# One written table orders all work of an attention and maxout-MoE kernel

## The chip, the cores and the metric

The kernel runs on one core of a Trainium2 chip. The core has five engines that run side by side, each with its own queue in program order: PE (TensorE, matmuls into PSUM), VectorE (DVE in the profile), ACT (ScalarE), POOL (GpSimd) and SP (SyncE, which here only issues DMAs). POOL can issue DMAs too, and those may change the type on the way. An instruction waits for semaphores of the others; whatever stands behind it on its engine waits with it. The metric is the device time of one execution in microseconds.

## The reference

```python
def _attn_ref(q, k, v):                 # (8 batches, 8 heads, 576 rows, 64)
    scores = (1 / np.sqrt(64)) * np.matmul(q, k.transpose(0, 1, 3, 2))
    mask = (pos[:, None] // 64) >= (pos[None, :] // 64)      # causal by blocks of 64
    attn = softmax(np.where(mask, scores, -1e9))
    return np.matmul(attn, v)

x = attn_out.transpose(0, 2, 1, 3).reshape(4608, 512)
h1, h2 = x @ w1, x @ w2                  # 512 -> 1024
out = np.maximum(h1, h2) @ w_out         # 1024 -> 512, float32
```

The kernel uses max(h1, h2) = relu(x (w1 - w2)) + x w2. So out = g w_out + x M with g = relu(x d), d = w1 - w2 and M = w2 w_out. M costs a small matmul of weights once; after that a row needs x d and one product of [x g] (1536 long) with [M; w_out].

## The kernel before, in words

**Attention** goes by pairs of heads, 32 pairs, two to a group. A group's q and k are loaded as fp32 (`load_qk`), cast to bf16 (`cast`), transposed on PE (`transposes`, 18 small ones) and copied out of PSUM to `qT` and `kT`. From group 6 on k comes by casting DMAs of POOL (`load_blocks`) and DMA transposes of SP (`transpose_blocks`). A pair's scores fill tiles of 2 x 512 columns in `ps_s` (two buffers of PSUM); ACT takes the exponential of each into `aT` (L568; L624 for a corner), POOL or VectorE sets masked corners to zero (`mask`, L573), and PE multiplies `aT` by `vv`, which holds v and a column of ones (`av`, L652). VectorE divides by the sum (L658, L659). The four pairs of the first batch are cut differently, in four pieces (`burst_p`, `burst_q1`, `burst_q2`, `burst_q3`), so that the first 256 rows are done early. The result is transposed into `xT` by PE (`x_out`) or, from group 4 to 14, by a DMA (`x_dma`).

**MoE** goes by spans of rows: 256, 320, seven of 512, and 448 (`spans`). For each span `h_unit` makes one of eight slices of x d, four matmuls into `ps_h`, drained through relu into `g` by VectorE or ACT. As spans do not end on 128 rows, `g` carries 64 columns over to the next span with a POOL copy (L236). The last step is a 2 x 2 block product of [x g] and [M; w_out], done with seven smaller `product`s of twelve matmuls each in place of eight. These need sums and differences of weights (`weight_sums`, L358) and of rows (`row_sums`, L364), kept in four `slot`s and in `bT_sb`; odd spans have a part of the row sums in a tile `xsum` of their own. VectorE makes all of them. `after` adds the results out of PSUM into `y` and stores them from SP.

**Weights.** `load_w` loads `moe_w1` (fp32) and `moe_w2` (to bf16) from POOL's queue, `diff_w` makes d on VectorE, `bT_unit` transposes `moe_w2` on PE, `m_unit` makes M.

**What sets the order.** Attention is written out by hand, in calls. MoE work stands in a list `units`; `fill(n)` runs the next steps of it whose rows are done, about n matmuls, at the places where the hand-written part calls it. Fixed rules place the drains: a unit's sums stand right behind it (`M_SUMS`, `G_SUMS`, `X_SUMS`). Every engine executes in the order in which the calls are made.

All tiles of MoE and of transposes share four PSUM buffers (`ps_m`).

Of the kernel before, what the change touches and what calls it, by code (L numbers as in the profile page):

```python
# [14 lines left out]
def kernel(  # L15
# [10 lines left out]
    nc = tc.nc  # L26
# [31 lines left out]
    QCUT = 256  # L58

    def a_col(p, c, t):  # L60
        if p >= HP:
            return CB[c] + t * P
        late = t * P >= QCUT
        return t * P + {
            0: 384 - QCUT if late else 0, 1: 704 - QCUT if late else 256 - P,
            2: 1024 - QCUT, 3: 1408 - 3 * P, 4: 1344 - 4 * P,
        }[c]


    SPAN = 512  # L70
    spans = [(0, QCUT), (QCUT, S - QCUT)]
    spans += [(t0, min(SPAN, NTOK - t0)) for t0 in range(S, NTOK, SPAN)]
    NSPAN = len(spans)


    FAST = 2
    carry = [t0 % P for t0, _ in spans]
    tiles = [(carry[i] + w) // P for i, (_, w) in enumerate(spans)]
# [34 lines left out]
    def load_qk(g, queues, gated=False):  # L113
        b, u = divmod(g, GPB)
        for nm, src, queue in (("q", q, queues[0]), ("k", k, queues[1])):
            if queue is None or by_dma(nm, g):
                continue
            raws[nm, g] = t = raw.tile([P, 2, RPP * D], FP32, name=f"{nm}raw")
            if gated:
                nc.gpsimd.memset(t[:, 0, :1], 0.0)  # L120
            queue.dma_start(
                out=t[:],
                in_=src[b, 4 * u:4 * u + 4].rearrange(
                    "(s h) (p t) d -> (h p) s (t d)", h=2, t=RPP),
            )

    T_DMA = {nm: 6 for nm in "k"}
    blk_n = {}

    def by_dma(nm, g):  # L130
        return g >= T_DMA.get(nm, NG)

    def load_blocks(nm, g):
        b, u = divmod(g, GPB)
        blk_n[nm, g] = n = raw.tile([P, S // BLK, 2, D], BF16, name=f"{nm}b", tag=f"{nm}raw")
        for h in range(2):
            for s in range(2):
                nc.gpsimd.dma_start(  # L138
                    out=n[h * BLK:(h + 1) * BLK, :, s],
                    in_=(q if nm == "q" else k)[b, 4 * u + 2 * s + h].rearrange(  # L140
                        "(j p) d -> p j d", p=BLK),
                )

    def transpose_blocks(nm, g):
        n = blk_n.pop((nm, g))
        for h in range(2):
            nc.sync.dma_start_transpose(
                out=(qT_r if nm == "q" else kT_r)[(2 * g + h) % NT].rearrange(
                    "q (j p) -> q j p", p=BLK),
                in_=n[h * BLK:(h + 1) * BLK].rearrange("p j s d -> p (j s d)"),  # L150
            )

    def cast(nm, g, parts):
        if by_dma(nm, g):
            return
        t = raws[nm, g].rearrange("p s (t d) -> p t s d", d=D)
        if (nm, g) not in qk_n:
            qk_n[nm, g] = qkn.tile([P, RPP, 2, D], BF16, name=f"{nm}n")
        n = qk_n[nm, g]
        for copy, j0, j1 in parts:  # L160
            copy(out=n[:, j0:j1], in_=t[:, j0:j1])  # L161
# [19 lines left out]
    def load_w(j, which=(0, 1)):  # L181
        fs = slice(j * WB, (j + 1) * WB)
        if 0 in which:
            w1_raw[j] = wraw.tile([P, NDM, WB], FP32, name="w1raw")
            nc.gpsimd.dma_start(out=w1_raw[j][:], in_=w1r[:, :, fs])
        if 1 in which:
            nc.gpsimd.dma_start(out=w2_sb[j], in_=w2r[:, :, fs])

    def diff_w(j):
        fs = slice(j * WB, (j + 1) * WB)  # L190
        nc.vector.tensor_sub(d_sb[:, :, fs], w1_raw[j][:], w2_sb[j])  # L191
# [8 lines left out]
    dve, pool, act = nc.vector.tensor_copy, nc.gpsimd.tensor_copy, nc.scalar.copy  # L200
    SP, ACT = nc.sync, nc.scalar
    warm = small.tile([P, 1], FP32, name="warm")
    load_qk(0, (SP, ACT))
    nc.vector.memset(warm[:], 0.0)
    zeros = wpool.tile([P, SPAN], BF16, name="zeros")
    nc.vector.memset(zeros[:], 0.0)
    nc.scalar.activation(out=warm[:], in_=warm[:], func=AF.Exp)
    load_qk(1, (SP, SP))
    load_qk(2, (SP, None))
    make_identity(nc, ident)  # L210
    for r in range(NV):
        nc.vector.memset(vv_r[r][:, :, :, D:D + 1], 1.0)
        nc.vector.memset(vv_r[r][:BLK, NCH - 1, :, :], 0.0)
    for r in range(NA):
        nc.vector.memset(aT_r[r][:, :, AW:], 0.0)
    for r in range(NT):
        nc.vector.memset(kz_r[r][:, BLK:2 * BLK], 0.0)
    cast("q", 0, ((dve, 0, 7), (pool, 7, RPP)))
    cast("k", 0, ((act, 0, 5), (dve, 5, RPP)))
    for c in range(2):  # L220
        load_v(0, c)
    load_w(0, (0,))
    cast("q", 1, ((pool, 7, RPP),))
    cast("k", 1, ((pool, 0, 7),))
    load_w(0, (1,))


    done_tokens = [0]
    g_tiles = {}

    def h_unit(i, f):
        if f == 0:
            g_tiles[i] = g_pool.tile([P, NFF, SPAN + BLK], BF16, name="g")
            if carry[i]:
                end = carry[i - 1] + spans[i - 1][1]
                nc.gpsimd.tensor_copy(  # L236
                    out=g_tiles[i][:, :, :carry[i]],
                    in_=g_tiles[i - 1][:, :, end - carry[i]:end])
        g = g_tiles[i]
        t0, w = spans[i]  # L240
        m = carry[i]
        pt = ps_m.tile([P, SPAN], FP32, name="ps_h", tag="m")
        for c in range(NDM):
            nc.tensor.matmul(  # L244
                pt[:, :w], d_sb[:, c, f * P:(f + 1) * P], xT[:, c, t0:t0 + w],
                start=(c == 0), stop=(c == NDM - 1),
            )
            if c == NDM - 1:
                if i >= FAST and on_act(i, f):
                    nc.scalar.activation(out=g[:, f, m:m + w], in_=pt[:, :w], func=AF.Relu)  # L250
                else:
                    nc.vector.tensor_scalar_max(g[:, f, m:m + w], pt[:, :w], 0.0)  # L252
                if i in (1, *range(FAST, NSPAN)) and f in X_SUMS:
                    row_sums(i, X_SUMS[f], 0)
            yield

    def bT_unit(j):
        pt = ps_m.tile([P, 2, NDM, P], BF16, name="ps_bT", tag="m")
        for i in range(2):
            for c in range(NDM):  # L260
                nc.tensor.transpose(pt[:, i, c, :], w2_sb[j][:, c, i * P:(i + 1) * P], ident[:])  # L261
                if i == 1 and c == NDM - 1:
                    (act if j % 2 else dve)(
                        out=bT_sb[:, 2 * j:2 * j + 2, :],
                        in_=pt.rearrange("p i c d -> p i (c d)"))
                yield

    def m_unit(i, c):
        ds = slice(i * WH, (i + 1) * WH)
        pt = ps_m.tile([P, WH], FP32, name="ps_M", tag="m")  # L270
        for f in range(NFF):
# [4 lines left out]
            if f == NFF - 1:  # L276
                nc.vector.tensor_copy(out=m_sb[:, c, ds], in_=pt[:])  # L277
                for k in M_SUMS[NDM * (1 - i) + c]:
                    weight_sums(k)
            yield  # L280

    def y_terms(i, s):
        g = g_tiles[i]
        t0 = spans[i][0] - carry[i] + s * P
        return [(xT[:, c, t0:t0 + P], m_sb[:, c]) for c in range(NDM)] + [
            (g[:, f, s * P:(s + 1) * P], wo_sb[:, f]) for f in range(NFF)]

    def y_unit(i, s):
        t0 = spans[i][0] - carry[i] + s * P
        py = ps_m.tile([P, d_model], FP32, name="ps_y", tag="m")  # L290
        terms = y_terms(i, s)
        for n, (lhs, rhs) in enumerate(terms):
            nc.tensor.matmul(
                py[:], lhs, rhs, start=(n == 0), stop=(n == len(terms) - 1),
            )
            if n == len(terms) - 1:
                y = y_pool.tile([P, d_model], FP32, name="y")
                nc.vector.tensor_copy(out=y[:], in_=py[:])
                nc.sync.dma_start(out=out[t0:t0 + P, :], in_=y[:])
            yield  # L300

    def y_last(i, s):
        t0 = spans[i][0] - carry[i] + s * P
        for m, w, copy, queue in ((0, 256, act, SP), (256, P, dve, SP), (384, P, act, ACT)):
            py = ps_m.tile([P, w], FP32, name="ps_y", tag="m")
            terms = y_terms(i, s)
            for n, (lhs, rhs) in enumerate(terms):
                nc.tensor.matmul(
                    py[:], lhs, rhs[:, m:m + w], start=(n == 0), stop=(n == len(terms) - 1),
                )  # L310
                if n == len(terms) - 1:
                    y = y_pool.tile([P, d_model], FP32, name="y")
                    copy(out=y[:, :w], in_=py[:])
                    queue.dma_start(out=out[t0:t0 + P, m:m + w], in_=y[:, :w])
                yield

# [12 lines left out]
    def a_parts(i, row, half):  # L329
        j, r = (row, 0) if i == 1 else (i, row)  # L330
        g, t0 = g_tiles[j], spans[j][0] - carry[j] + 2 * r * P
# [605 lines left out]
```

## Time and profile before

| what | value |
|---|---|
| median of 3 runs | 248.3 us (247.65 to 248.72) |
| the profiled execution | 247.61 us, its span 245.8 us |
| busy: PE, VectorE, ACT, POOL | 234.4, 185.4, 143.8, 129.6 us |
| granted TensorE clock | 0.997 |
| instructions in the trace | 7595 |

The span runs from the first to the last instruction of the program. Busy time is a union: matmuls are pipelined, so one that takes 273 ns may start 109 ns after the one ahead. Idle time in the groups has the releaser beside it, the instruction that ended the wait. PEld is the weight load ahead of a matmul. The chain that ended last goes back from the last instruction, at each step to what released it.

### The profile page before, as it was taken

What the parts mean: (1) busy time and instruction counts of PE and PEld (TensorE: products, weight loads), DVE (VectorE), ACT (ScalarE), POOL (GpSimd) and SP (SyncE); (2) the same over time, 40 slices, a digit from 0 to 9 for tenths busy, and PEclk for the clock granted to TensorE, in tenths of its full rate; (3) what the DMA queues carried; (4) which work ended last, traced back from release to release, by engine and by line L of the source; (5) the groups of instructions that cost most, each with busy time, mean ns of one, the idle gap of its engine ahead of it and who ended that gap; (6) DMA issues with size and microseconds to landing.
All of it is one profiled execution on the core that took longest, in us unless ns stands there. A gap on an engine that the chain in (4) does not pass through costs nothing.

```text
span 245.8 us, 7595 instructions
## 1 busy us (share of the span) xinstructions
PE 234.4 (95%) x3093; PEld 167.3 (68%) x3109; DVE 185.4 (75%) x395; ACT 143.8 (58%) x200; POOL 129.6 (53%) x294
## 2 busy tenths in 40 slices
PE   7689899999999999999999999999999999999993
PEld 2347666688865886588558755875587578567782
DVE  4976989999677958795879587957785788526573
ACT  2888871677677748673867386748673730462200
POOL 1996952669959584948593859485621210010000
PEclk9999999999999999999999999999999999999998
DMA  6999999579999999999999999999994321301125
GB/s 233 318 206 306 231 278 195 172 137 188 153 196 180 168 163 222 184 201 183 244 227 130 208 164 272 122 223 193 134 138 97 100 39 45 131 0 43 47 86 172
DMA packets 108867, 41.33 MB, mean 168 GB/s; under 512 B 89248, under 2 KB 102688, under 8 KB 108832
## 3 DMA queue, kind: packets, MB, share of 16 engines
q0 software_dynamic: 65952, 11.87, 69.4%
q1 hardware_dynamic: 42464, 28.32, 51.7%
q10 hardware_dynamic: 416, 0.66, 0.8%
q8 instruction: 24, 0.39, 0.7%
q14 instruction: 11, 0.09, 0.1%
HBM read 34.60 MB, written 9.44 MB: 179 GB/s over the span
## 4 chain that ended last, share of the span: by engine, by line
PE 87%; DVE 7%; ACT 4%; issue 1%; ACTq 0%
PE ps_p L390 35%; PE ps_h L244 24%; PE ps_o L652 11%; PE ps_s L544 9%; PE ps_w L514 3%; ACT aT L568 3%; PE ps_qT L525 2%; DVE sums L358 2%; DVE sums L364 1%; DVE g L252 1%; DVE m_sb L277 1%; PE ps_s L562 1%; PE ps_xe L690 1%; PE ps_bT L261 1%; DVE qT L533 1%
## 5 line engine op out<-in xcount | busy, mean ns | idle before, releaser
L568 ACT ACTIVATE aT<-ps_s 128x1024 bf16<-128x1024 f32 (+2 forms) x100 | 95.7, 994 | 32.1 <-PE ps_s L544 24.0
L244 PE MATMUL ps_h<-xT,d_sb 128*128 128x512 bf16 (+3 forms) x307 | 68.0, 357 | 1.0 <-DVE d_sb L191 0.3
L573 POOL MEMSET aT<- 64x128 bf16 x124 | 21.8, 200 | 52.8 <-ACT aT L568 51.9
L244 PEld LDWEIGHTS <-d_sb 128*128 128x128 bf16 x320 | 29.7, 98 | 26.7 <-issue 2.2
L652 PEld LDWEIGHTS <-aT 128*128 128x128 bf16 x960 | 37.2, 98 | 6.9 <-issue 0.8
L652 PE MATMUL ps_o<-vv,aT 128*128 128x65 bf16 x960 | 39.8, 194 | 0.3 <-DVE xp L659 0.3
L250 ACT ACTIVATE g<-ps_h 128x512 bf16<-128x512 f32 (+1 forms) x40 | 23.3, 587 | 23.3 <-PE ps_h L244 22.3
L165 POOL DMA_DIRECT2D vv<-in_v_dram x40 | 33.9, 857 | 1.1 <-issue 0.9
L252 DVE TENSOR_SCALAR g<-ps_h 128x512 bf16<-128x512 f32 (+2 forms) x40 | 23.6, 594 | 13.1 <-PE ps_h L244 12.8
L659 DVE TENSOR_TENSOR xp<-ps_o,rec 128x256 bf16<-128x256 f32 (+1 forms) x64 | 31.4, 491 | 2.2
L544 PE MATMUL ps_s<-qT,kT 64*128 64x64 bf16 (+6 forms) x344 | 31.3, 280 | 1.8 <-ACT kT L533 0.7
L390 PE MATMUL ps_p<-sums,bT_sb 128*128 128x256 bf16 x216 | 32.8, 273 | 0.0
L390 PEld LDWEIGHTS <-bT_sb 128*128 128x128 bf16 x288 | 27.5, 98 | 4.5 <-issue 1.4
L138 POOL DMA_DIRECT2D kb<-in_k_dram x40 | 29.5, 765 | 0.0
L533 ACT COPY qT<-ps_qT 128x576 bf16<-128x576 bf16 (+1 forms) x17 | 10.3, 614 | 23.2 <-PE ps_qT L525 23.2
L390 PEld LDWEIGHTS <-g 128*128 128x128 bf16 x220 | 19.8, 98 | 4.8 <-issue 2.8
L390 PE MATMUL ps_p<-wo_sb,g 128*128 128x256 bf16 (+1 forms) x148 | 22.7, 270 | 0.0
L161 POOL CAST qn<-qraw 128x1152 bf16<-128x1152 f32 (+1 forms) x16 | 17.1, 1067 | 5.1 <-DMA qraw<-in_q_dram 5.1
L544 PEld LDWEIGHTS <-kT 64*128 64x128 bf16 x344 | 12.2, 94 | 10.5 <-issue 5.1
L658 DVE RECIPROCAL rec<-ps_o 128x4 f32<-128x4 f32 (+1 forms) x64 | 11.8, 184 | 6.8 <-PE ps_o L652 6.8
L236 POOL COPY g<-g 128x512 bf16<-128x512 bf16 x8 | 5.9, 733 | 20.6 <-ACT g L250 20.3
L364 DVE TENSOR_TENSOR bT_sb<-g 128x1024 bf16<-128x1024 bf16 x18 | 12.4, 688 | 5.4 <-ACT g L250 4.8
(90 smaller groups left out, 326.1 us busy)
## 6 DMA issues: line engine op xcount, KB each, us to landing
qraw<-in_q_dram SPq DMA_DIRECT2D x16, 576.0 KB, 6.0
out_dram<-y SPq DMA_DIRECT2D x35, 256.0 KB, 3.9
vv<-in_v_dram POOLq DMA_DIRECT2D x32, 128.0 KB, 7.3
kraw<-in_k_dram SPq DMA_DIRECT2D x5, 576.0 KB, 7.4
kb<-in_k_dram POOLq DMA_DIRECT2D x40, 72.0 KB, 6.8
w1raw<-in_moe_w_dram POOLq DMA_DIRECT2D x4, 512.0 KB, 8.8
xT<-in_moe_w_dram POOLq DMA_DIRECT2D x4, 256.0 KB, 9.2
wo_sb<-in_moe_w_out_dram POOLq DMA_DIRECT2D x2, 512.0 KB, 10.9
```

What stands on the lines that cost most here:

```text
L138: nc.gpsimd.dma_start(out=n[h * BLK:(h + 1) * BLK, :, s], in_=(q if nm == "q" else k)[b, 4 * u + 2 * s + h].rearrange("(j p) d -> p j d", ...
L161: copy(out=n[:, j0:j1], in_=t[:, j0:j1])
L165: nc.gpsimd.dma_start(out=vv_r[b % NV][P - rows:, c, :, :D], in_=v[b, :, c * P:c * P + rows, :].rearrange("h p d -> p h d"),)
L244: nc.tensor.matmul(pt[:, :w], d_sb[:, c, f * P:(f + 1) * P], xT[:, c, t0:t0 + w], start=(c == 0), stop=(c == NDM - 1),)
L250: nc.scalar.activation(out=g[:, f, m:m + w], in_=pt[:, :w], func=AF.Relu)
L252: nc.vector.tensor_scalar_max(g[:, f, m:m + w], pt[:, :w], 0.0)
L390: nc.tensor.matmul(pt[:, q0:q0 + w], lhs[c][:, s * P:(s + 1) * P], rhs[c][:, m:m + w], start=(c == 0 and q0 == 0), stop=(c == 5 and q0 + w ...
L544: nc.tensor.matmul(ps[:, hh, col:col + w], kT[r, k0:k0 + P], qT[r, q0:q0 + w], start=True, stop=True,)
L568: nc.scalar.activation(out=aT_r[p % NA][:, :, a0:a0 + w], in_=ps[:, :, :w], func=AF.Exp, scale=scale,)
L573: (eng or nc.gpsimd).memset(aT_r[p % NA][BLK:, :, a0:a0 + BLK], 0.0)
L652: nc.tensor.matmul(po[:, gi, hh, :], a[:, hh, a0:a0 + P], vv[:, c, h0 + 2 * hh, :], start=(mm == 0), stop=(mm == n_mm - 1),)
L659: nc.vector.tensor_mul(xp[:, :, ts[0]:ts[0] + n, p % 2].rearrange("q s t d -> q t s d"), po[:, :, :, :D], rec[:, :n].to_broadcast([P, n, 2 ...
```

## The change

The two hand-written parts, `units`, `fill` and `plan` are gone. All work stands in one table, `SCHEDULE`, of 945 words, and each word issues one step:

- L, K, V, u, v, o: loads of q or k, of k blocks, v, `moe_w1`, `moe_w2`, `w_out`; C a cast, T transposes, c their copy, J a DMA transpose of k
- S a score tile, E its exponentials and masks, A the `aT` matmuls, N the normalisation, X and I the transposes of x by PE and by DMA
- B, D, M: transposes of `moe_w2`, a difference of weights, a unit of M; W and R sums of weights and of rows (`R8_40`: span 8, sum 4, its first part)
- H and Y: the next so many matmuls of h, and twice so many of the products; z warm-ups, m memsets

The letter behind a colon is the engine (D VectorE, P POOL, A ACT, N: no gate ahead of a load).

The order among the units changes: `moe_w2` and `w_out` are loaded and M is made ahead of `moe_w1`, whose loads go to SP's queue. There are nine spans of 512 rows, with no carry. All pairs use three score tiles. Row sums have one buffer (`xsum` is gone). Of 84 instructions that make sums of weights and rows, counting `diff_w`, 32 go to POOL; casts are spread over ACT, VectorE and POOL; masks go to VectorE or POOL word by word. Normalisations and copies out of PSUM no longer follow their matmuls at once.

```diff
-    QCUT = 256
-    spans = [(0, QCUT), (QCUT, S - QCUT)]
-    spans += [(t0, min(SPAN, NTOK - t0)) for t0 in range(S, NTOK, SPAN)]
-    carry = [t0 % P for t0, _ in spans]
+    NSPAN = NTOK // SPAN
...
-            nc.gpsimd.dma_start(out=w1_raw[j][:], in_=w1r[:, :, fs])
+    def load_w1(j, gate=None):
+        w1_raw[j] = t = wraw.tile([P, NDM, WB], FP32, name="w1raw")
+        if gate is not None:
+            gate.memset(t[:, 0, :1], 0.0)
+        nc.sync.dma_start(out=t[:], in_=w1r[:, :, j * WB:(j + 1) * WB])
...
-            g_tiles[i] = g_pool.tile([P, NFF, SPAN + BLK], BF16, name="g")
-            if carry[i]:
-                nc.gpsimd.tensor_copy(
-                    out=g_tiles[i][:, :, :carry[i]],
-                    in_=g_tiles[i - 1][:, :, end - carry[i]:end])
+            g_tiles[i] = g_pool.tile([P, NFF, SPAN], BF16, name="g")
...
-    def row_sums(i, n, k):
+    def row_sums(i, n, k, eng):
+        sub, add = eng.tensor_sub, eng.tensor_add
...
+    SCHEDULE = """
+        z14 V0_2 Cq0a:A V0_1 V0_4 Lq1:N mz2:D v1 V0_3 v2 Lk1:D Cq0b:A Tq0 cq0_0:A Ck0a:D Ck0b:P Tk0 cq0_1:A
+        V0_0 ck0_0:D Z0 ck0_1:D z1 S0_1 Z1 Cq1a:D mk:P Cq1b:P S1_0 S0_0 E0_1:D z3 S0_2 v3 Tq1 cq1_0:D S1_2 v0
+        o1 ma:P z3 S1_1 Ck1a:D mo1:P Ck1b:P Tk1 E0_0:D ck1_0:D cq1_1:D E1_0:D B1:D Lk2:P E1_2:P E0_2:P E1_1:P
+        S2_0 ck1_1:A Z3 Z2 S2_1 mo0:D z3 S3_0 mz0:P E2_0:D E2_1:D B2:D E3_0:P o0 mo2:D S3_1 E3_1:P A0a A0b N0a
+        N0b A1a N1a A2a N2a S3_2 S2_2 E3_2:P Ck2a:D Lq2:D Lk3:P A1b N1b u0:N u1:D u2:D E2_2:P Cq2a:P B0:A
+        Ck3a:P A3b N3b B3:D A2b N2b X0:AA M12:D Ck2b:D M10:A Tk2 ck2_0:D Z4 mz1:D ck2_1:A Cq2b:A M13:D M11:A
+        Tq2 cq2_1:D D0:P Z5 A3a N3a M03:D cq2_0:A S4_1 u3:N Ck3b:A S5_0 E5_0:P Tk3 ck3_1:D V1_0 D2:P M00:D S4_0
+        Lq3:N E4_0:P X1:DD D1:D V1_1 M02:A E4_1:D H9 D3:D W1:D K6_0 W3:D ck3_0:A V1_4 S4_2 Lk4:N Cq3a:P W2:D
...
+        R7_10:P Y3 H3 Y2 H5 R7_11:D R7_21:D H1 R7_20:P H1 Y1 R7_30:P Y14 H1 Y2 H3 R7_40:D H5 Y3 H6 R7_41:P Y9
+        H1 Y1 H1 Y2 H3 Y3 R7_31:P R8_10:D R8_20:P Y4 H4 Y5 H1 R8_30:P H1 Y1 H3 R8_11:D R8_21:D Y12 R8_31:D Y8
+        R8_41:D Y10 R8_40:D Y15
+    """
...
+    def step(token):
+        name, _, o = token.partition(":")
...
+        elif kind == "E":
+            exps(*n, ENGINE[o])
+        elif kind == "A":
+            av(n[0], PARTS[rest[-1]])
+        elif kind == "N":
+            normalize(n[0], PARTS[rest[-1]])
...
+        elif kind == "R":
+            row_sums(n[0], *divmod(n[1], 10), ENGINE[o])
+        elif kind == "H":
+            for _ in range(n[0]):
+                next(h_work)
+        elif kind == "Y":
+            for _ in range(2 * n[0]):
+                next(y_work)
...
+    for token in SCHEDULE.split():
+        step(token)
```

## The prediction

> **What bounds the kernel now.** I read the busy line first, then busy time by stages, the chain that ended last, the groups by shape, one tile's rows and the DMA issues.
>
> ```profile
> PE 234.4 (95%) x3093; PEld 167.3 (68%) x3109; DVE 185.4 (75%) x395; ACT 143.8 (58%) x200; POOL 129.6 (53%) x294
> ```
>
> The stages (us busy of PE, PEld, DVE, ACT, POOL, then clock, DMA share, GB/s) say where PE is not full:
>
> ```profile
> 0.00:30.00 30.00, 24.66 (x402) 14.69 (x405) 22.46 (x62) 21.15 (x31) 22.24 (x46) 1.00 1.27 261
> 30.00:38.00 8.00, 7.51 (x74) 5.68 (x75) 7.22 (x17) 5.33 (x7) 5.03 (x13) 1.00 1.48 251
> 38.00:52.00 14.00, 13.15 (x227) 10.04 (x226) 13.83 (x32) 6.61 (x9) 5.27 (x15) 1.00 1.06 194
> 80.00:180.00 100.00, 99.58 (x1358) 70.96 (x1359) 77.06 (x159) 67.55 (x92) 66.86 (x154) 1.00 1.78 189
> 180.00:230.00 50.00, 49.84 (x509) 35.85 (x510) 32.13 (x66) 20.52 (x32) 5.56 (x17) 1.00 0.27 67
> 230.00:241.80 11.80, 11.78 (x109) 10.04 (x107) 9.36 (x16) 1.67 (x3) 0.00 (x0) 1.00 0.29 97
> ```
>
> From 52 us to its last matmul at 241.8 PE never stands still at full clock; another order of the same matmuls can only lose there. What can be won lies before 52 us, where waits stand between the matmuls (24.66 busy still holds 5.7 us of matmuls on zeros). The chain, in order of time:
>
> ```profile
> 23.00 1.94 ACT aT L568 x2
> 24.94 0.64 ACT kT L533
> ...
> 45.05 1.03 DVE sums L358 x2
> 46.54 0.42 DVE xp L659
> 47.33 1.12 DVE sums L358
> ...
> 203.99 0.74 PE ps_o L652 x24
> ...
> 210.95 7.18 PE ps_h L244 x33
> 218.13 1.31 PE ps_p L390 x12
> ...
> 232.60 9.20 PE ps_p L390 x90
> ```
>
> Until 25 us ACT's exponentials lead, until 50 us VectorE (the sums of weights), then PE to the end. The rows price a PE unit: 0.218 for a 512-wide matmul of h, 1.31 for a product of twelve, 0.92 for a pair's 30 matmuls on `aT`; starts in the timeline give 0.84 for a pair's scores and 0.27 for a group's 18 transposes. Durations and landings:
>
> ```profile
> L568 ACT ACTIVATE aT<-ps_s 128x1024 bf16<-128x1024 f32 x92 | 90.9, 1023 | 31.1 <-PE ps_s L544 22.9 <-PE ps_s L562 7.6
> L161 POOL CAST qn<-qraw 128x1152 bf16<-128x1152 f32 x14 | 16.2, 1160 | 0.6 <-DMA qraw<-in_q_dram 0.6
> L443 DVE TENSOR_TENSOR y<-ps_p,y 128x512 f32<-128x512 f32 x9 | 6.1, 681 | 0.0
> L364 DVE TENSOR_TENSOR sums<-sums,xT x5: 424/856/1354, 37.4 to 212.2; 128x512 bf16<-128x512 bf16 x5
> qraw<-in_q_dram SPq DMA_DIRECT2D x16, 576.0 KB, 6.0
> wo_sb<-in_moe_w_out_dram POOLq DMA_DIRECT2D x2, 512.0 KB, 10.9
> ```
>
> **Ledger.** Products, `aT` matmuls, M and transposes keep their number. h goes from 320 to 288 matmuls over the same columns, warm-ups from 29 to 24; these change nothing where PE is full. Four exponentials fewer but each 512 wide, with four corner ones more: 5.1 us removed, 5.2 added. The eight carry copies (5.9 us on POOL) and most of POOL's casts go, hidden before since POOL is 53% busy; ACT takes casts instead, some 16 us over the run. Thirty sums and two differences go to POOL. All DMAs stay in number; the four of `moe_w1` move from POOL's queue to SP's.
>
> **Start, followed by hand.** (1) Three loads of v and two of `moe_w2` now run before q0 and k0 land (5.8 and 6.3 us in the timeline): 0.9 MB beside 1.15 MB. Sharing evenly at the 295 GB/s of the first 10 us costs up to 0.5 MB, 1.7 us; if they do not collide, nothing. I take 1.0. (2) Without it: casts 5.9 to 7.2, transposes and copies to 9.1, first exponential 9.5. Pairs 0 to 3 need twelve of 1.02 and four of 0.27, 13.4 us; with two score buffers and the listed order ACT waits about 2.2 us for PE (the second tile of pair 1 waits behind that of pair 0) and copies once, so the last ends near 25.8; the copy of `bT` follows, 26.8, and the transposes of x end PE's attention part at 27.5. Then M. The kernel before ended these exponentials at 26.0, so nothing is won yet. (3) q2's load waits for a VectorE memset that now stands behind four normalisations and a cast, near 25.4; on SP k3 and all four loads of `moe_w1` are queued behind it. q2 at 6.0 us lands at 31.4, cast 32.2; each further 0.5 MB about 1.4 later (q and k of before land 6.0 and 7.4 after issue): `moe_w1` from 34.2 to 38.4. The first half of `moe_w_out` is issued behind POOL's masks at 22.4 and lands at 33.3 (10.9). So M runs 27.5 to 31.2, waits for q2 and then for that half, and five more M units, scores and transposes end near 37.5, where h can start: its first difference on POOL is done by 36.3. Had no load held it, the 8.1 us of units from 27.5 would end at 35.6. (4) At 37.5 the units done are 18.4 us (four pairs, 7.0; four more score tiles, 1.1; seven transposes, 1.9; `bT` 1.8; seven M, 6.1; x, 0.5).
>
> By 52.3 the kernel before had done 30.5 us of units (h 7.9, M 7.0, `bT` 1.8, transposes 2.7, six pairs 10.5, x 0.6), and 31.1 by 52.9. The new kernel reaches 31.1 at its third product (6 in the list), 12.7 of units after 37.5. That product reads the sum `R0_21`, and from 37.5 to this sum VectorE's queue holds 14.7 us: two differences 2.4, four h drains 2.8, five W sums 2.9, five R sums 2.9, two normalisations 1.2, a copy and a cast 1.4, a drain 0.7, masks. So 52.2 where units alone give 50.2: M ahead of `moe_w1` wins 0.7 us against 52.9.
>
> **Middle.** Over the next 14 us of units VectorE has 1.7 us more work than PE, and ACT has 17.7 in 17.4 between the exponentials of pairs 6 and 11, with score tiles waiting on two buffers. Both fall into one stretch: 1.3 together (0 if the lag is absorbed, 3.5 if not). Beyond, all engines stay below PE over any 10 us.
>
> **Sums on POOL.** No row shows POOL with two inputs. From below: one input of 1152 in 1.16, so 1.03 for 1024. From above: its copy of 512 at 0.73, doubled for size and for inputs, 2.9. I take twice the cast, 2.0. Six of these sums stand 2.0 to 2.6 us of PE units ahead of the product that reads them, so 2.0 costs 0.5 in all, 2.9 about 4, 1.03 nothing. What is queued behind them is masks and loads of v, which have several us. The Trainium skill (GPSIMD Engine Reference, sections 3.1 Elementwise and 8 Key points) has POOL 1.96 times slower than VectorE for two inputs, 4497 ns for 2048 fp32, and a shared SBUF interface that contends with VectorE's two-input instructions. By it 1024 would take an estimated 2.25, and the late sums 1 to 2 us. The tile row above shows the same contention: a 512 sum takes 424 alone and 1354 at 37.4, beside POOL's cast.
>
> **Tail.** In the last span the new VectorE order has the sum `R8_40` behind both adds of product 7, and the very next product, 3, reads it with its first matmul. PE ends product 7 and waits: 0.15 to the add, 0.69, 0.68, 0.42 for the sum, 0.1: 2.0 us. Before, this sum was made during h, and the last 90 matmuls run unbroken. No load or engine covers it. The end from the last matmul, 4.0 us, is the same.
>
> **Other bubbles.** An order fixed to one list meets landings and drains that differ from it; nothing in the trace prices this. Nothing at best, 6 us at worst (0.2 for each of 30 pairs); the 0.15 to 0.4 us that PE loses in any 50 us now is the nearest row, and I take 1.0.
>
> **Sum.** Span 245.8 - 0.7 (start) + 1.0 (q0) + 1.3 (middle) + 0.5 (POOL) + 2.0 (tail) + 1.0 = 250.9. The profiled execution took 247.61 for 245.8, so 252.7; the median of the runs, 248.3, lies 0.7 above it: 253.4.
>
> **Rivals.** *It fills as meant.* With loads on time (-1.9) and ACT's 2.2 of waits closed to 0.7 (-1.5) h starts at 34.1; q0 is not delayed (-1.0), VectorE's surplus is absorbed (-2.0 and -1.3), POOL and bubbles cost nothing (-1.5): span 241.7, time 244.2. For it: M's 7.0 us stand exactly where PE waits for ACT. Against: the SP queue behind q2. It is faster once 6.3 of these 9.2 us are won; h starting before 34.5 decides it. 0.18. *Even.* Half of them: 248.8; 0.12. *POOL's sums and bubbles.* If 1024 takes 2.9, or VectorE and POOL hold each other up in the sums, +3.5, and bubbles 5: 253.4 + 7.5 = 260.9. For it the 1354 row, against it POOL's idle half; 0.2. *Forecast*, 0.5.
>
> **Numbers.** The likeliest is 253.4, its own range 250 to 257. Eight in ten reach into the fast rival and nearly to the slow one: 246.5 to 261. A change under 0.5% (1.2 us) can't be told from none: the runs of before span 1.07. Faster than 247.1: 0.18; within: 0.12; slower than 249.5: 0.70.
>
> **What would show it.** First matmul of h at 37.5 (wins if before 34.5); third product at 52; q2 landing past 31, `moe_w1` to 38; PE's gap of 2.0 us before product 3, some 6.6 us from the end, released by VectorE's sum; POOL's sum rows at 2.0; PE full between 60 us and the tail. Wrong if PE is unbroken there or if the loads land earlier.

## The result, and the profile after

The changed kernel takes 256.13 us (median of 4 runs, 253.56 to 256.81), the kernel before 248.5 us (247.65 to 248.72) on the same chip. The ratio is 1.0295, with a 95% interval of 1.0219 to 1.037: slower by 7.6 us. The profiled execution's span is 255.0 us where that of before was 245.8, so 9.2 us are to be found in the traces.

The busy line and the stages of the changed kernel (us busy of PE, PEld, VectorE, ACT, POOL with the number of instructions, then granted clock, DMA share, GB/s):

```profile
PE 236.8 (93%) x3040; PEld 162.1 (64%) x3064; DVE 175.2 (69%) x386; ACT 153.6 (60%) x213; POOL 155.4 (61%) x263
```

```profile
0.00:30.00 30.00, 24.84 (x382) 15.29 (x384) 16.67 (x45) 21.32 (x30) 17.43 (x48) 1.00 1.28 240
30.00:38.00 8.00, 7.95 (x112) 5.29 (x105) 6.64 (x12) 6.24 (x10) 6.75 (x9) 1.00 1.08 367
38.00:52.00 14.00, 9.42 (x92) 4.93 (x91) 10.68 (x19) 10.31 (x17) 13.13 (x19) 0.86 1.50 230
52.00:60.00 8.00, 7.78 (x126) 5.98 (x125) 6.36 (x14) 4.45 (x6) 2.69 (x6) 0.82 0.64 127
80.00:180.00 100.00, 98.89 (x1285) 67.01 (x1295) 70.84 (x159) 67.90 (x92) 72.63 (x123) 1.00 1.55 171
180.00:230.00 50.00, 48.94 (x540) 34.30 (x543) 34.95 (x72) 21.44 (x32) 23.30 (x27) 1.00 0.68 100
230.00:251.00 21.00, 19.16 (x160) 15.16 (x161) 11.51 (x19) 3.99 (x7) 2.96 (x3) 1.00 0.19 64
```

The kernel before from 52 to 60 us, and two groups of the changed kernel:

```profile
52.00:60.00 8.00, 7.98 (x152) 6.60 (x149) 7.76 (x18) 6.39 (x10) 7.46 (x14) 1.00 0.95 143
```

```profile
L181 PE MATMUL ps_h<-xT,d_sb 128*128 128x512 bf16 x266 | 70.0, 379 | 1.3 <-DVE xT L505 0.2
L181 PEld LDWEIGHTS <-d_sb 128*128 128x128 bf16 x288 | 27.1, 98 | 23.4 <-issue 1.2
```

The span grew by 9.2 us, of which 2.4 are PE busy longer (236.8 against 234.4) and 6.8 are PE standing still. The split is a little rough: of the 288 matmuls of h 22 have no record in this trace (13 of 320 in that of before), and the place of a missing one shows as idle. Until 38 us the new order is as good as the old one, slightly better (idle 0.05 us instead of 0.49 from 30 to 38). Then comes the loss: from 38 to 52 us PE stands still 4.58 us where it was 0.85, which is 3.7 of the 6.8. The same stretch and the one behind it show a granted clock of 0.86 and 0.82, where before it was 1.00: there matmuls take longer, which is where PE is busy longer. The end (230 to 251) stands still 1.84 us, where before it lost nothing. From 52 to 230 us (52 to 60, 60 to 80 and the two stages above) the idle time shown grew by 0.2 to 0.9 us a stage, 2.2 in all; little of that is the order's, as the first experiment shows.

The chain that ended last, in order of time (start, us, what), shows what leads into the loss:

```profile
24.32 7.46 DMA w1raw<-in_moe_w_dram
...
31.93 1.01 POOL d_sb L161
...
35.58 2.13 POOL d_sb L161
...
37.99 11.48 DMA vv<-in_v_dram
...
49.51 0.32 PE ps_o L464 x3
```

POOL makes two differences of weights as soon as `moe_w1` has landed, and the loads of v for batch 1 stand behind them in its queue. The one issued at 37.99 us takes 11.48 us to land, and PE stands until 49.5 us. PE's timeline (start, us, instruction, and in brackets the wait and its releaser):

```profile
46.59 0.42 PE L376 MATMUL ps_kT<-ident,kn 64*128 64x64 bf16 x17 [1.93 <-DVE g L189]
...
49.51 0.32 PE L464 MATMUL ps_o<-vv,aT 128*128 128x65 bf16 x3 [1.87 <-DMA vv<-in_v_dram]
49.65 0.61 PE L282 MATMUL ps_p<-m_sb,xT 128*128 128x256 bf16 x2
50.06 1.06 PE L282 MATMUL ps_p<-wo_sb,g 128*128 128x256 bf16 x4
```

Two waits of 1.9 us stand close together. The second is the late v. The first is a drain of h on VectorE, held by this row of VectorE's timeline:

```profile
43.09 2.25 DVE L131 CAST kn<-kraw 128x512 bf16<-128x512 f32 x1
45.26 0.68 DVE L262 TENSOR_TENSOR bT_sb<-g 128x1024 bf16<-128x1024 bf16 x1
45.86 0.68 DVE L189 TENSOR_SCALAR g<-ps_h 128x512 bf16<-128x512 f32 x1
```

Here the cast runs beside a sum and two DMA issues of POOL, from 42.94 to 45.88, and takes 2.25; the drain behind it comes late. A cast of the same shape takes 0.42 us at 27.04, where POOL stands idle. In the runs below this one takes 2.25 again in the two that leave v's loads and POOL's sums as they are here, and 0.41 to 0.48 in all others. Whether the sum or the issues stretch it is not shown apart. And after the two waits, four products of 256 columns take 1.06 us (50.06) where four take 0.60 elsewhere: PE runs at half clock. The windows that show it:

```profile
44.62:48.03 3.41, 1.09 (x27) 0.56 (x26) 2.95 (x5) 1.46 (x4) 3.29 (x7) 1.00 1.49 221
48.03:54.85 6.82, 5.34 (x32) 3.85 (x32) 3.12 (x10) 2.80 (x4) 3.43 (x6) 0.50 1.44 155
```

The clock was granted at half for 6.83 us, right after a stretch of 3.41 us in which PE was busy for 1.09. The Trainium skill (TensorE: Matmul & The Clock Gate, Part 1) describes an activity window of 3413 ns that runs freely and halves the clock after an idle one. Length, ratio and whole multiples agree with the rows. That the window has to be idle does not: this one held 1.09 us of matmuls.

The tail, from the timeline of PE and VectorE, is as the prediction drew it, with a wait of 1.73 us for 2.0:

```profile
246.82 0.68 DVE L333 TENSOR_TENSOR y<-ps_p,y 128x512 f32<-128x512 f32 x1
247.42 0.68 DVE L335 TENSOR_TENSOR y<-ps_p,y 128x512 f32<-128x512 f32 x1
248.02 0.42 DVE L262 TENSOR_TENSOR sums<-xT,sums 128x512 bf16<-128x512 bf16 x1
248.49 0.39 PE L282 MATMUL ps_p<-m_sb,sums 128*128 128x256 bf16 x2 [1.73 <-DVE sums L262]
```

### The profile page after: what moved, and what is told of

The parts are those of the page before. It is cut to its first block, busy times and chain, and to the rows that moved or that the text cites. A ratio compares the mean times of both kernels' runs of the same rounds, so it can differ in the third digit from the quotient of the medians.

```text
span 255.0 us, 7458 instructions
## 1 busy us (share of the span) xinstructions
PE 236.8 (93%) x3040; PEld 162.1 (64%) x3064; DVE 175.2 (69%) x386; ACT 153.6 (60%) x213; POOL 155.4 (61%) x263
## 4 chain that ended last, share of the span: by engine, by line
PE 69%; ACT 8%; DMA 7%; DVE 7%; issue 4%; POOL 3%; POOLq 0%; SPq 0%; DVEq 0%
PE ps_p L282 27%; PE ps_h L181 21%; PE ps_o L464 9%; PE ps_s L394 6%; ACT aT L418 6%; DMA vv<-in_v_dram 5%; DMA w1raw<-in_moe_w_dram 3%; PE ps_w L365 3%; PE ps_qT L376 1%; POOL d_sb L161 1%; DVE bT_sb L262 1%; PE ps_s L412 1%; ACT aT L441 1%; DVE xp L476 1%; DVE y L333 1%
## 5 line engine op out<-in xcount | busy, mean ns | idle before, releaser
L418 ACT ACTIVATE aT<-ps_s 128x1024 bf16<-128x1024 f32 x96 | 95.3, 1025 | 30.5 <-PE ps_s L394 28.4
L181 PE MATMUL ps_h<-xT,d_sb 128*128 128x512 bf16 x266 | 70.0, 379 | 1.3 <-DVE xT L505 0.2
L423 POOL MEMSET aT<- 64x128 bf16 x81 | 15.2, 205 | 51.8 <-ACT aT L418 47.4
L187 ACT ACTIVATE g<-ps_h 128x512 bf16<-128x512 f32 x40 | 23.8, 598 | 36.6 <-PE ps_h L181 35.2
L394 PE MATMUL ps_s<-qT,kT 64*128 64x448 bf16 (+4 forms) x320 | 31.6, 288 | 2.7 <-ACT aT L418 1.3
L476 DVE TENSOR_TENSOR xp<-ps_o,rec 128x384 bf16<-128x384 f32 (+1 forms) x64 | 31.4, 491 | 2.2
L189 DVE TENSOR_SCALAR g<-ps_h 128x512 bf16<-128x512 f32 x32 | 21.7, 686 | 10.3 <-PE ps_h L181 9.9
L282 PE MATMUL ps_p<-sums 128*128 128x256 bf16 x108 | 20.6, 273 | 0.3
L475 DVE RECIPROCAL rec<-ps_o 128x6 f32<-128x6 f32 (+1 forms) x64 | 11.8, 184 | 10.3 <-PE ps_o L464 9.8
L394 PEld LDWEIGHTS <-kT 64*128 64x128 bf16 x320 | 10.7, 94 | 12.2 <-issue 9.5
L262 POOL TENSOR_TENSOR sums<-xT 128x512 bf16<-128x512 bf16 x11 | 13.0, 1180 | 8.6 <-PE ps_p L282 8.4
L282 PEld LDWEIGHTS <-sums 128*128 128x128 bf16 x144 | 13.1, 98 | 7.5 <-issue 2.7
L384 DVE COPY qT<-ps_qT 128x576 bf16<-128x576 bf16 x18 | 13.3, 753 | 4.0 <-PE ps_qT L376 3.8
```

What stands on the lines that cost most here:

```text
L181: nc.tensor.matmul(pt[:], d_sb[:, c, f * P:(f + 1) * P], xT[:, c, t0:t0 + SPAN], start=(c == 0), stop=(c == NDM - 1),)
L187: nc.scalar.activation(out=g[:, f], in_=pt[:], func=AF.Relu)
L189: nc.vector.tensor_scalar_max(g[:, f], pt[:], 0.0)
L262: op(s_parts(i, n)[k], get(x)[k], get(y)[k])
L282: nc.tensor.matmul(pt[:, q0:q0 + w], lhs[c][:, s * P:(s + 1) * P], rhs[c][:, m:m + w], start=(c == 0 and q0 == 0), stop=(c == 5 and q0 + w ...
L394: nc.tensor.matmul(ps[:, hh, col:col + w], kT[r, k0:k0 + P], qT[r, q0:q0 + w], start=True, stop=True,)
```

## The experiments

Each run is compared with the kernel before on the same chip; the ratios are to that. Runs that stand under different headings ran on different chips in part, where the kernel before took 247.6 to 248.5 us, so differences of 1 or 2 us between them need a second look. The theory at the start: the loss has two separate parts, the tail (2 us) and the late loads of v around 45 us (5 to 6 us, with the clock that they cost). The rivals: the sums on POOL are the cause, or something else stands right behind the v loads and takes their place.

### The sum at the tail

```diff
-        R8_11:D R8_21:D Y12 R8_31:D Y8
-        R8_41:D Y10 R8_40:D Y15
+        R8_11:D R8_21:D R8_40:D Y12
+        R8_31:D Y8 R8_41:D Y10 Y15
```

> One word of the table moved: the sum R8_40 stands right behind R8_21 on VectorE, ahead of the adds of the last products. Theory (this sum, late in VectorE's order, keeps PE waiting before product 3): the wait of 1.73 us and its idle of 1.82 us between 230 and 251 us go, 1.8 us less than the changed kernel, about 254.3 us. Rival (the adds are what the end waits for, so the wait only moves to the last adds): 0 to 0.5 us less.

Measured: 254.15 us (253.47 to 255.13), ratio 1.025 [1.0196, 1.0304], 2.0 us less than the changed kernel. The two intervals overlap; the clean measure is the pair of runs below that differ in this edit alone on one chip, 254.74 without it and 252.59 with it: 2.15 us. The gap is gone. This profile, in which no matmul lacks its record, also settles the middle, where the words are the same:

```profile
80.00:180.00 100.00, 99.46 (x1291) 66.97 (x1288) 70.81 (x160) 67.85 (x92) 72.40 (x122) 1.00 1.50 172
180.00:230.00 50.00, 49.87 (x548) 34.59 (x546) 34.02 (x71) 21.48 (x32) 23.57 (x27) 1.00 0.52 98
```

PE stands still 0.54 and 0.13 us, where the profile of the changed kernel had 1.11 and 1.06. From 60 to 230 us it is 0.75 us in all, against 0.73 in the kernel before: the order shows no cost there. The changed kernel's own profile has 2.7 us: the same 0.75, one pause of 0.72 us at 181.44 for which it names no releaser, and some 1.2 us that fit the missing records.

### The loads of v ahead

```diff
-        E2_2:P Cq2a:P
+        E2_2:P V1_0 V1_1 V1_4 V1_2 V1_3 Cq2a:P
```

The five words leave their places behind POOL's differences and sums.

> The five loads of v of batch 1 (V1) stand on POOL's queue ahead of the cast that waits for q2, so also ahead of the two differences of weights. Theory (late V1 loads keep PE idle around 47 to 49.5 us, and the idle lowers the granted clock until 59 us): PE's idle time in 38 to 52 us, 4.58 us, falls to about 1 as in the kernel before, the granted clock stays at 1.0, and the time falls by 5 to 6 us, to about 250.5. Rival (VectorE's queue of sums, casts and drains holds PE there, v only comes on top): the wait for v goes but PE waits for VectorE instead, at most 1.5 us less.

Measured: 254.74 us (254.5 to 255.64), ratio 1.0278 [1.0228, 1.0328]: 1.4 us won, where 5 to 6 were expected. By the medians alone that is not clear of noise; on one chip, on top of the edit at the tail, the same words win 1.56 us (254.15 to 252.59). The wait for v is gone, and the clock stays at 1.00. But the idle time of PE from 30 to 60 us falls only from 4.85 to 3.81 us. Now PE waits 2.35 us for a drain of h on VectorE, which waits for a difference of weights, which waits for `moe_w1` (PE's row, then VectorE's):

```profile
44.10 0.44 PE L376 MATMUL ps_qT<-ident,qn 64*128 64x64 bf16 x18 [2.35 <-DVE g L189]
```

```profile
39.56 1.23 DVE L161 TENSOR_TENSOR d_sb<-w1raw,xT 128x1024 bf16<-128x1024 f32 x1 [2.13 <-DMA w1raw<-in_moe_w_dram]
```

q2 landed 0.6 us later than in the changed kernel and the four blocks of `moe_w1` 1.2 to 2.8 us later, with v issued beside them. Nor did all of v gain: the five loads, issued at 24.2 to 27.7 us, take up to 25.6 us, and the last two land at 50.5 and 53.3, where the changed kernel, issuing them at 42.9 and 45.0, has them at 51.8 and 52.8. The theory was half right: without the late v the clock stays up, but it hid another wait.

### All sums on VectorE

```diff
-        D0:P
+        D0:D
...
-        R0_10:P
+        R0_10:D
```

and so for all 32 sums and differences that POOL makes.

> All 32 sums and differences of POOL go to VectorE, at the same places of the table. Theory (POOL's sums, 2.1 us for 1024 and contending with VectorE's, cause the V1 delay and the small gaps in the middle): POOL's queue is free for the V1 loads sooner, PE idle from 60 to 230 us falls from 2.7 towards 0.7, 3 to 6 us less than the changed kernel. Rival (VectorE is the scarcer engine and 20 us more on it show): same or up to 4 us more.

Measured: 256.92 us (256.66 to 259.69), ratio 1.0384 [1.0309, 1.0459]: no gain. POOL falls to 106.3 us busy, VectorE rises to 186.6. The idle time moves to 30 to 38 us, 3.95 us (D0 and D2 now wait for `moe_w1` in VectorE's queue, and the drains of M behind them), and from 38 to 52 only 0.64 is left. So trading POOL's sums for 11 us more on VectorE does not cure the loss; what they cost apart from that the run does not show. The stall does not stay where it was: here it goes to the queue that now has the wait for `moe_w1`.

### Both edits

The words of the first and second experiments together.

> The two moves together, V1 loads earlier and R8_40 earlier. If both theories hold and do not meet (one at 45 us, one at 246 us), the gains add: 7 to 8 us less than the changed kernel, 248 to 249, level with the kernel before. If V1 is not the cause, 2 to 3 us less.

Measured: 252.59 us (252.29 to 252.7), ratio 1.0182 [1.0127, 1.0237]. The two gains add up (3.5 us against the changed kernel). From 30 to 60 us 4.68 us of idle time are left (1.36 in the kernel before). The waits of that stretch point at `moe_w1`. VectorE's difference at 40.53 us waited 2.07 us for it, POOL's at 34.12 and 38.45 waited 1.25 and 1.71, and PE waited 2.29 us for the drain behind. If `moe_w1` is late, loading it sooner should win.

### The loads of moe_w1 ahead

On top of both edits (first), and on the changed kernel alone (second):

```diff
-        Lk2:P
+        Lk2:P u0:N u1:N u2:N u3:N
...
-        A1b N1b u0:N u1:D u2:D E2_2:P
+        A1b N1b E2_2:P
...
-        S4_1 u3:N Ck3b:A
+        S4_1 Ck3b:A
```

> The kernel of e4_tail_v1 with one more edit: the four loads of moe_w1 are issued right behind the load of k of group 2, ahead of the loads of q2 and k3, without memsets in front, instead of behind them. In e4_tail_v1 (median 252.59, TensorE idle 4.68 us between 30 and 60 us of the span, 1.36 in the kernel before) the differences wait for moe_w1 to land (2.07 us on VectorE, 1.25 and 1.71 on GpSimd) and the drains behind D3 hold TensorE 2.29 us. Theory (late moe_w1 is what is left of the stall): those waits go, the idle between 30 and 60 falls by about 3 us to 1.5 or 2, and the median comes to about 249.5. Rival (the DMA queues are full either way, so that what is loaded later, q2, k3 and v, is late instead): the idle between 30 and 60 stays above 3.7 and the median within 1 us of 252.6, with waits on q2, k3 or v in place of moe_w1.

> The changed kernel with one edit alone: the four loads of moe_w1 right behind the load of k of group 2, ahead of q2 and k3, without memsets; the loads of v of batch 1 stay behind GpSimd's differences and sums. Theory (two separate causes: late moe_w1 and late v): the differences start some 2 to 4 us sooner, and v of batch 1, which lay in the DMA queues behind moe_w1's 2 MB and was issued behind the differences, lands sooner too; TensorE's idle of 4.58 us between 38 and 52 us falls to about 2, the granted clock of 0.86 rises, and the median falls by 2.5 to 4 us to about 252 to 253.5. Rival (the late issue of v on GpSimd alone holds the attention of batch 1): the wait for vv at about 49 us stays within 1 us of where it is, and the median falls by under 1 us.

Measured: 259.13 us (258.7 to 259.61), ratio 1.0424 [1.0327, 1.052], and 260.6 us (259.91 to 261.44), ratio 1.049 [1.0406, 1.0574]. Both are slower, by 6.5 and 4.5 us, against every expectation. PE's timeline of the first:

```profile
36.63 0.66 PE L376 MATMUL ps_qT<-ident,qn 64*128 64x64 bf16 x18 [5.73 <-POOL qn L131]
```

q2, issued at 23.2 us behind 2 MB of `moe_w1` on the same queue, landed at 35.7. What was late is now early, and what was in time is late.

### Which load goes first

If the order on SP's queue were all, q2 ahead of `moe_w1` and both early would do. Three orders, all on top of both edits: q2 and then `moe_w1`; q2 alone; and q2 early with `moe_w1` on POOL's queue, as the kernel before has it. The words leave their old places; the lines below show this only in part.

```diff
-        Lk2:P
+        Lk2:P Lq2:N u0:N u1:N u2:N u3:N
```

> The kernel of e4_tail_v1 with the load of q2 and then the four of moe_w1 issued right behind the load of k of group 2, all without memsets in front. In e5_w1_tail_v1 moe_w1 went first on SyncE's queue and the load of q2, issued at 23.2 us, landed at 35.7 us: TensorE stood 5.7 us for it and the median was 259.13. Theory (the order on SyncE's queue, and the memset that holds q2 until 23 us, decide): q2 is issued at about 15 us and lands by 23, moe_w1 lands by 32, GpSimd's casts of q2 and all differences start 2 us or more sooner than in e4_tail_v1 (30.1, 34.1), idle between 30 and 60 us falls from 4.7 to under 3 and the median to 250 to 251.5. Rival (the DMA engines are full from 14 to 40 us in any order, so that w_out, k3 or v of batch 1 is late in their place): the median stays at 252 or above, with a wait of over 1 us on wo_sb, k3 or vv.

```diff
-        Lk2:P
+        Lk2:P Lq2:N
...
-        Ck2a:D Lq2:D Lk3:P
+        Ck2a:D Lk3:P
```

> The kernel of e4_tail_v1 with the load of q2 alone moved right behind the load of k of group 2, without its memset; moe_w1 stays where it is, behind k3. Theory: q2 lands some 6 us sooner (its cast ended TensorE's wait of 1.29 us at about 31 us), moe_w1 has 0.6 MB less in front of it from 23 us and lands 1 to 2 us sooner; idle between 30 and 60 us falls from 4.7 to about 3, the median to 251 to 251.8. Rival (moe_w1 is bound by the packets of v and w_out on GpSimd's queue, not by q2): the first wait goes but the wait for the differences grows by as much, the median stays at 252.3 to 253.

```diff
-        o1 ma:P
+        o1 u0:N u1:N u2:N u3:N ma:P
...
-        nc.sync.dma_start(out=t[:], in_=w1r[:, :, j * WB:(j + 1) * WB])
+        nc.gpsimd.dma_start(out=t[:], in_=w1r[:, :, j * WB:(j + 1) * WB])
```

> The kernel of e8_q2 with the four loads of moe_w1 issued by GpSimd on its own queue right behind the first half of w_out (about 13 to 17 us), as the kernel before issues them on GpSimd's queue at 8 to 20 us, instead of by SyncE at 24 to 30 us. Theory (moe_w1 behind q2 and k3 on SyncE's queue is what makes it late; a queue of its own has it there by 30 us as in the kernel before): the differences start by 30 us instead of 34, the waits for moe_w1 go, idle between 30 and 60 us falls to 1.5 to 2.5 and the median to 249.5 to 251. Rival (the load is late because the DMA engines are full, whichever queue): TensorE waits 1 us or more for q2, the second half of w_out or v instead, and the median stays at 252 or above.

Measured: 258.49 us (257.99 to 259.69), ratio 1.0432 [1.0375, 1.0488]; 251.35 us (251.29 to 252.76), ratio 1.0154 [1.011, 1.0199]; 261.85 us (260.89 to 262.46), ratio 1.0561 [1.0515, 1.0606]. The waits of PE (what waited and for whom, us in total, times, longest), first those of the order q2, `moe_w1`, then those with `moe_w1` on POOL:

```profile
PE ps_kT L376 <- POOL kn L131: 3.6, 1, 3.6
PE ps_M L207 <- DMA wo_sb<-in_moe_w_out_dram: 1.9, 1, 1.9
```

```profile
PE ps_M L207 <- DMA wo_sb<-in_moe_w_out_dram: 5.7, 1, 5.7
```

With q2 and `moe_w1` early, k3 is late (issued at 22.9, landed at 37.9 us) and so is `w_out`. With `moe_w1` on POOL's queue the second half of `w_out` lands 16.4 us after its issue, at 40.0 us, and M waits 5.7 us. Its other wait, 3.5 us until 17.2, ends after POOL's memsets of `aT`, which stand behind the four issues and run at 16.29 us (12.95 with the loads on SP's queue). The bytes say why. From the GB/s of the stages, the kernel before has moved 9.8 MB by 38 us, the changed one 10.1, and all these orders 9.1 to 10.3 (the one with `moe_w1` on POOL 10.3). No order has moved much more by then; each chooses which load is late. The kernel before issues `moe_w1` from 8 to 20 us and `w_out` only at 24 us, which only M needs, and M stands behind the first two spans of h. With M ahead of h, `w_out`, q2, k3 and `moe_w1` are all needed between some 27 and 40 us. An order with M behind h in the table was not run; that this alone would cure it stays argued. There is a second candidate that no run tests. Between 28.4 and 33.0 us SP issues five loads of q and k of later groups, 0.6 MB each, where the kernel before issues its next two at 38.5 and 39.0; by 60 us the changed kernel has moved 14.4 MB, the kernel before 13.7. These loads are on their way when v of batch 1 is late, and none was held back.

Only q2 alone gains, 1.2 us: issued at 15.2 instead of 23.2 us, it takes its 0.6 MB out of the stretch, and `moe_w1` lands 2.1 us sooner. The intervals of the two ratios overlap, so the gain is not clear of noise; the profiles' spans differ by the same 1.2 us (250.7 and 249.5). With 251.35 us this is still 1.5% behind the kernel before, and no version of the table that was run beats it.

### What is left: VectorE around 42 us

In that best version PE's wait is the drain of h's third unit. VectorE's timeline:

```profile
38.45 1.23 DVE L161 TENSOR_TENSOR d_sb<-w1raw,xT 128x1024 bf16<-128x1024 f32 x1 [1.36 <-DMA w1raw<-in_moe_w_dram]
39.59 1.29 DVE L254 TENSOR_TENSOR sums<-wo_sb 128x1024 bf16<-128x1024 bf16 x2
40.80 0.94 DVE L254 TENSOR_TENSOR sums<-m_sb 128x512 bf16<-128x512 bf16 x1
41.66 0.68 DVE L254 TENSOR_TENSOR sums<-sums,wo_sb 128x1024 bf16<-128x1024 bf16 x1
42.26 1.27 DVE L189 TENSOR_SCALAR g<-ps_h 128x512 bf16<-128x512 f32 x2
```

and PE's, with the window that shows what the wait costs beyond itself:

```profile
42.99 0.44 PE L376 MATMUL ps_qT<-ident,qn 64*128 64x64 bf16 x18 [1.83 <-DVE g L189]
...
43.61 4.02 PE L181 MATMUL ps_h<-xT,d_sb 128*128 128x512 bf16 x10
```

```profile
40.44:43.85 3.41, 1.57 (x32) 0.75 (x31) 3.31 (x8) 2.98 (x6) 3.10 (x4) 1.00 1.21 336
43.85:47.26 3.41, 3.41 (x10) 1.19 (x8) 2.79 (x5) 2.30 (x4) 3.18 (x8) 0.50 1.21 335
```

Difference and sums stand ahead of the drain. The wait of 1.83 us leaves PE 1.57 of 3.41 us busy, and for the next 3.41 us the clock is halved: ten matmuls of h take 4.02 us, which at 0.218 each is 2.2. Two ways to take the drain out from behind the sums:

```diff
-        H9 D3:D W1:D K6_0 W3:D ck3_0:A S4_2 Lk4:N Cq3a:P W2:D S5_1 E5_1:P M01:A W4:P Lq4:N W5:D H3 Cq3b:A H1
-        R0_10:P H9
+        H9 K6_0 ck3_0:A S4_2 Lk4:N Cq3a:P S5_1 E5_1:P M01:A Lq4:N H3 Cq3b:A H1
+        D3:D H9
...
-        Ck4b:D R0_31:D
+        Ck4b:D R0_10:P W1:D W3:D W2:D W4:P W5:D R0_31:D
```

> The kernel of e8_q2 with VectorE's and GpSimd's queues reordered between 38 and 50 us and nothing else: the difference D3, which waited 1.36 us for the last block of moe_w1 on VectorE, stands behind the drain of the third unit of h, and the sums of weights W1, W3, W2, W4, W5 stand behind the casts and copies of q3 and k4 instead of right behind D3. In e8_q2 that drain ran at 42.26 us, behind D3 and 2.9 us of sums, and TensorE waited 1.83 us for it; the granted clock was 0.88 from 38 to 52 us. Theory (what is left of the stall is VectorE's queue order around the late moe_w1): the wait of 1.83 us goes, the clock stays near 1.00, and the median falls from 251.35 by 1.8 to 3 us to 248.3 to 249.5, within 1 percent of before. Rival (VectorE is full there, 12.2 of 14 us, so that the sums moved behind are late for the drains, copies or products after them): TensorE waits as long between 44 and 56 us, and the median stays at 251 or above.

```diff
     def on_act(i, f):
-        return i >= 8 or f % 2 == 1
+        return i in (0, 8) or f % 2 == 1
```

> The kernel of e8_q2 with all eight drains of h of the first span on ScalarE, where four of them are VectorE's (2.6 us less on VectorE between 36 and 48 us, 2.4 us more on ScalarE, which was busy 10.6 of 14 us from 38 to 52). In e8_q2 the drain of the third unit stood behind D3 and the sums on VectorE and TensorE waited 1.83 us for it; moving the sums back instead (e10_drain) moved the waits back and cost 2.5 us. Theory (VectorE is the full engine of the stretch, and what it is relieved of comes off): the wait goes, the clock of 0.88 in 38 to 52 rises to 0.95 or more, and the median falls from 251.35 by 1.5 to 3 us to 248.3 to 249.9. Rival (ScalarE's exponentials and casts behind the drains come late in their place, or ScalarE's own wait for q3 holds a drain): TensorE waits for aT, kn or g of ScalarE, and the median stays at 250.8 or above.

Measured: 253.87 us (253.67 to 255.37), ratio 1.0258 [1.0226, 1.0289], and 251.29 us (251.23 to 251.48), ratio 1.0145 [1.0122, 1.0168]. Both rivals held. In the first the wait of 1.83 us is gone, but 46 to 52 us is worse. VectorE's timeline there:

```profile
45.52 1.64 DVE L254 TENSOR_TENSOR sums<-sums,wo_sb 128x1024 bf16<-128x1024 bf16 x1
47.08 1.64 DVE L262 TENSOR_TENSOR bT_sb<-g 128x1024 bf16<-128x1024 bf16 x1
...
49.73 1.62 DVE L262 TENSOR_TENSOR bT_sb<-g 128x1024 bf16<-128x1024 bf16 x1
```

The sums that were moved back meet POOL's sums (45.31 to 48.16) and its casts and DMA issues. One of them and two row sums behind it (`bT_sb`) take 1.64, 1.64 and 1.62 us instead of 0.68. PE then waits 1.78 us for a normalisation behind them, and its idle time from 38 to 52 us is 4.13 us. In the second, PE's waits between 20 and 60 us are six of 0.16 to 0.94 us, four of them released by ACT, and the clock is halved once more, from 46.88 to 50.29 us: what was taken off VectorE came back, in the main, as late copies and drains of ACT. In these three versions VectorE is 11.5 to 12.2 us busy of the 14 from 38 to 52, ACT 10.4 to 11.7, POOL 10.0 to 10.7.

### POOL's sums in the old order

On the kernel before, the first part of each of the four row sums of a span goes to POOL. It is 36 instructions (POOL has 330 instead of 294), not the 28 of the expectation:

```diff
+        sub, add = (nc.gpsimd if k == 0 else nc.vector).tensor_sub, (nc.gpsimd if k == 0 else nc.vector).tensor_add
```

> The kernel before with one edit alone: the first four row sums of every MoE span (row_sums with k = 0, 28 instructions of 512 elements per partition) on GpSimd instead of VectorE. It prices the sums on GpSimd without the new order. My account of the prediction charged 0.5 us for GpSimd's sums in the changed kernel; the changed kernel with all 32 sums on VectorE (e3_dve) was 0.8 us slower than it, within its interval. Theory (GpSimd's sums cost little by themselves; the order and the late loads are the cause): 247.5 to 249, within 0.5 percent of before. Rival (a sum of 1.15 us on GpSimd in place of 0.42 us on VectorE comes late for its product, or slows VectorE beside it): above 250, with products that wait for GpSimd's sums.

Measured: 256.07 us (254.79 to 256.58), ratio 1.0298 [1.0214, 1.0382]: slower by 8.3 us, as much as the whole change. The rival held. The waits of PE and a piece of the chain:

```profile
PE ps_p L391 <- POOL xsum L365: 3.3, 2, 1.8
PE ps_p L391 <- POOL sums L365: 2.9, 3, 1.2
```

```profile
129.63 1.98 POOL vv L165 x3
131.97 2.98 POOL kb L138 x4
134.95 1.18 POOL sums L365
```

By this piece of the chain the 1.18 us of the instruction are not what costs most. In the old order the sums stand on POOL behind 5 us of DMA issues for v and k, and the products need them at once; POOL holds 27% of the chain that ended last. In the changed kernel PE has no listed wait that a sum of POOL ends, and moving the sums off POOL wins nothing. That the places of the sums in the table make this difference is likely, but no run shows it by itself.

## Why the prediction was right, and where it was not

The sign held, and 256.1 measured lies inside the likeliest case's own range of 250 to 257 around 253.4. The tail was seen as it is. That the number fits is otherwise luck in good part: the largest loss, 6.3 us between 38 and 60, has no term in the sum, and three terms that do stand there, q0, middle and bubbles, 3.3 us together, show 0.3 us outside that stretch. The steps, in the prediction's order:

**Start.** h was to begin at 37.5 us, with q2 landing past 31 and `moe_w1` from 34.2 to 38.4. It began at 34.49. q2 was issued at 23.40 (25.4 in the prediction) and landed 5.3 us later (6.0), so it was cast at 28.84; the first block of `moe_w1` was there by 31.9, the last by 36.8. The forecast was 1.6 to 2.7 us late, 2.0 of it from the place of the memset ahead of q2 and little from the landing times. The prediction itself named earlier loads as a sign that it is wrong, and here it was.

**The prediction's main miss** stands in its paragraph on POOL's sums: "masks and loads of v, which have several us". The loads of v did not. The chain shows v of batch 1 issued at 37.99 and landing 11.48 us later, and the third product, forecast for 52.2, began at 55.9. From 38 to 60 us the kernel lost 3.9 us of idle time and 2.4 of clock, 6.3 us, where the prediction had no term for the stretch but a share of "other bubbles". The first theory of its cause, late v alone, fell too: moving v ahead gave 1.4 to 1.6 us, since `moe_w1` stood right behind.

**The clock** had no term. PE pauses of about 2 us were priced at their own length, but the two that stand close together were followed by 6.83 us at half clock, which cost 2.4 us more.

**q0** delayed by v and `moe_w2`: 1.0 forecast, 0.3 measured (first transposes at 7.23 us, 6.95 before).

**Sums on POOL**: 2.0 us for 1024 elements forecast, 2.12 measured (1.15 for 512). The estimate of 2.25, half of the 4497 ns that the Trainium skill gives for 2048 fp32 (GPSIMD Engine Reference, section 3.1 Elementwise), is 6% above the row. As late sums they cost nothing that the profile shows: no wait of PE is listed as ended by one. The run that moved all of them to VectorE won nothing, but it loaded VectorE in exchange and does not price them. The contention that the prediction saw in a row of 1354 ns is there, and larger: 0.41 to 2.25 for a cast, 0.68 to 1.64 for a sum. The Trainium skill (GPSIMD Engine Reference, section 1 Specifications) names VectorE's instructions with two SBUF inputs, or in a two-port mode, as those that contend with GpSimd. The sum is one of these and agrees; the mode of the cast no row shows.

**Tail**: 2.0 us forecast, a wait of 1.73 in the profile, 2.15 between the two runs on one chip that differ in this edit alone. This step held, place, releaser and size.

**Middle and bubbles**: 1.3 and 1.0 forecast. From 60 to 230 us neither is to be seen: 0.75 us idle in the complete profile of the same words, 0.73 before. For the middle that is the lower bound that the prediction named.

**The rival that ended faster** was to be decided by h starting before 34.5 us. It started at 34.49, and the kernel was slower all the same. The deciding point was chosen too early: M ahead of h does fill the wait of 23 to 30 us, but it makes `w_out` due earlier, in the stretch of the other loads, and the loss comes behind the start of h. How much of it M's place causes stays open. **"Even"** is excluded by the interval. **"POOL's sums and bubbles"** had the mechanism of VectorE and POOL holding each other up; that part was seen, at 43.09.

## What to carry to other kernels

When a reorder brings the user of a load forward, add up the bytes that all users in that stretch need, and those that are loaded ahead for later, and compare them with what the queues have moved by then: where they do not fit, moving one load ahead makes the next one late (four of six such moves cost 4.5 us or more, the other two won 1.2 to 1.6). An engine's instruction is cheap or dear by what stands ahead of it in its queue, not by its own time: taking the sums off POOL won nothing in one order, and giving POOL sums cost 8.3 us in the other. Check that a profile has all its matmuls before reading small idle times from it. Price a pause of the matmuls not only by its length but also by the clock that follows, and look at two pauses that stand within a few us of each other as one.

## What was not expected of the hardware

The clock is halved in whole pieces of 3.41 us (3.41 or 6.83) after a window in which PE was busy for part of the time. Counted back from each drop, in eight profiles, the window of 3.41 us ahead of it held 0.00 to 1.75 us of PE work (1.09 in the changed kernel, 1.57 and 1.75 in the two versions with q2 alone early; the trace with 1.75 lacks some matmuls). Windows with 2.0 us and more never led to a drop. Placed by the other clock events of their traces, a window with some 1.5 us in the run with v ahead, one with 1.66 in the run with all sums on VectorE and one with 1.60 in the run with sums on POOL in the old order did not lead to one either. So between some 1.5 and 1.75 us both were seen, and what decides there stays open. In the run with the drain ahead of the sums, PE stood still as much, but its windows held 2.13 and 2.02 us, and the clock stayed:

```profile
47.62:51.03 3.41, 2.13 (x18) 1.51 (x16) 3.41 (x4) 2.90 (x4) 3.41 (x6) 1.00 1.08 111
51.03:54.45 3.42, 2.02 (x40) 1.37 (x40) 3.15 (x10) 1.12 (x2) 2.07 (x3) 1.00 1.04 72
```

A load on a busy queue lands late beyond its size: 0.6 MB of q2 took 12.5 us behind 2 MB of `moe_w1` on the same queue, 0.5 MB of `w_out` 16.4 us behind `moe_w1` on POOL's.
